# A delta-rule scan with a routed feed-forward: key products in two PSUM banks of their own, a new order of work in a slot

## Chip, cores and metric

The kernel runs on one core of one Trainium2 chip. The metric is the device time of the whole kernel in microseconds; the median of the runs counts. Before the change it is 1098.14 us (three runs, 1096.19 to 1109.95).

## The reference

Three parts follow one another. Only the first one is touched by the change.

```python
# 1. delta rule: 4 batches x 8 heads, 768 steps, head size 48
k_n = k / (norm(k) + 1e-06)
for t in range(S):
    y[:, :, t] = q[t] @ state
    state = state + beta[t] * outer(k_n[t], v[t] - state^T k_n[t])
# 2. top-1 routed feed-forward: 3072 rows of 384, 8 experts of 1024
e = argmax(x @ w_gate); out = softmax_e * (relu(x @ w1[e]) @ w2[e])
# 3. gated unit: (sigmoid(x @ w_gate) * (x @ w_val)) @ w_out, width 1536
```

## The kernel before

All is float32, and matrix products run on PE as several passes. The delta rule is done in chunks: 768 steps are 12 chunks of 64 steps, and 32 (batch, head) pairs lie two by two on the 128 partitions, 16 pairs along the free axis. In each chunk the recurrence is a triangular system of 64 by 64 per pair. It is cut into two blocks of 32 by 32 that are inverted by elimination, and a product that joins them.

Two chunks make a **group** (g = 0 to 5), and each chunk is done in two halves of 8 pairs, so a group has four **slots** (sl = 0 to 3) and the loop of `run` has k = 0 to 25 slots: 24 of the scan and 2 that only finish. The names in the rows:

- `norm(g)` (L83): ACT squares the keys (`sq`), DVE sums them (`n`) and makes `nrm`, `gam`, `ngam` in 17 small instructions.
- `Gd` (L109) and `Gq` (L120): the **key products**, keys with keys (`gd`, 128 matmuls in the trace for a chunk) and keys with queries (`gq`, 64). DVE scales them out of PSUM into `ado` and `atq`, at the place in DVE's order where the call stands.
- `sys`, `lower` (L131, L133): DVE transposes `ado` into `asys`, POOL masks it. `elim` (L138): the elimination, 30 steps of a multiply (L144) and an add (L146). For group 0 DVE does all; for the others POOL does the first 26 and DVE the last JD = 4. `back` (L148) is these last steps and two transposes on DVE, `tn` and `r`.
- `merge` (L157): `mp` and `mr` on PE, copies `pp` and `rt` on ACT, and four copies of the diagonal blocks of `rt` (L181).
- The scan's own steps in slot k: `z_` (PE `zps`, then DVE `z`), `u_` (PE `ups`, then ACT `u` in 8 instructions), `s_` of the slot before (PE `sps`, then DVE adds into the state `S`), `yb` and `ya` (PE `yps`). `rows` (ACT copies the output to `xrow`, a ring of 8), `turn` (PE `xT`, ACT `xt`) and `gate` (PE `lgp`, DVE `lg`) prepare the router.
- `Route.route` (L356) routes four slots at a time: small DVE instructions, `rank` on PE, a scale of each `xrow` on ACT (L396), and on POOL an indirect DMA of each `xrow` to `xs` (L402). Each waits for the one before it to land. It is a generator, moved on by `ra` at three places in a slot.

Each engine works its instructions in the order in which they are written; `pt` moves POOL's elimination on by four instructions at a time, between the other calls. PSUM has eight banks: two for `yps` and six (`ps_m`) that all other products share.

Loads go out on ACT's queue, one or two in a slot. In slot 21 `free_early` gives memory to the weights of the second part, and after the loop the routed part (from about 396 us) and the gated unit keep PE busy to the end.

## Time and profile before

| | |
|---|---|
| median of three runs | 1098.14 us |
| profiled execution, its own time | 1107.87 us |
| its span, first to last instruction | 1106.1 us |
| PE busy in the span | 998.9 us (90%) |
| DVE, ACT, POOL busy | 545.4, 381.3, 373.4 us |
| PE's share of the chain that ended last | 80% |
| granted TensorE clock, mean over the span | 0.900 of full speed |

The clock that is granted to TensorE has two levels here, 1.2 and 2.4 GHz; a row of the stretches gives its mean as a share of 2.4 GHz, so 0.50 is the lower level all the time and 1.00 the upper. A busy PE at the lower level does about half the work, so busy time alone does not tell how fast it is. Times inside the execution are counted from the start of the span.

### The profile page before, as it was taken

The numbers are of one execution on the slowest core, as the hardware profiler recorded it, in microseconds if no ns is written. First come the engines' busy times: TensorE is split into PE (matmuls) and PEld (weight loads), VectorE is DVE, ScalarE is ACT, GpSimd is POOL, SyncE is SP. The second block draws the span as 40 slices with busy tenths as digits, with TensorE's granted clock in tenths as the row PEclk, the third lists the DMA queues.
The fourth block names the chain that finished last, engine by engine and source line by source line (L and its number), as shares of the span: only waits on it lengthen the run. The fifth ranks groups of instructions, "written<-read, shape, count | busy, mean of one in ns | idle before, by whom it ended". The sixth has DMA issues, their size and how long they took to land.

```text
span 1106.1 us, 25856 instructions
## 1 busy us (share of the span) xinstructions
PE 998.9 (90%) x11330; PEld 913.5 (83%) x11330; DVE 545.4 (49%) x1032; ACT 381.3 (34%) x746; POOL 373.4 (34%) x435
## 2 busy tenths in 40 slices
PE   2366989898898899999999999999999999999994
PEld 2355988898797789999999988888888888888894
DVE  6845383747322357656653155553366553343331
ACT  1041526162543344444444433333322222222221
POOL 2048847385701255555566601000010000011211
PEclk8587797878856689999999999999999999999997
DMA  8142132222200164576655312111021100000010
GB/s 316 69 165 80 57 113 82 97 77 72 75 31 31 44 215 130 150 193 195 168 140 161 96 40 76 58 39 48 12 74 58 58 20 1 1 36 29 36 43 32
DMA packets 32029, 94.46 MB, mean 85 GB/s; under 512 B 4168, under 2 KB 12072, under 8 KB 31912
## 3 DMA queue, kind: packets, MB, share of 16 engines
q1 hardware_dynamic: 21384, 61.51, 18.5%
q10 hardware_dynamic: 6624, 21.77, 5.9%
q0 software_dynamic: 3904, 9.47, 2.4%
q8 instruction: 91, 1.49, 0.6%
q14 instruction: 26, 0.21, 0.1%
HBM read 70.90 MB, written 21.84 MB: 84 GB/s over the span
## 4 chain that ended last, share of the span: by engine, by line
PE 80%; DVE 7%; POOL 5%; issue 3%; DMA 2%; ACT 1%; SPq 0%; POOLq 0%; ACTq 0%; DVEq 0%
PE gps L556 5%; PE ops L555 5%; PE gps L557 5%; PE vps L556 5%; PE ops L557 5%; PE vps L555 5%; PE vps L557 5%; PE ops L556 5%; PE gps L555 5%; PE yps L192 4%; PE hps L557 3%; PE hps L555 3%; PE yps L555 3%; PE hps L556 3%; PE yps L556 3%; PE yps L557 3%
## 5 line engine op out<-in xcount | busy, mean ns | idle before, releaser
L472 POOL TENSOR_TENSOR wl<-raw,wh 128x1536 fp32r<-128x1536 f32 x31 | 108.9, 3513 | 82.1 <-ACT wh L471 82.0
L732 DVE TENSOR_TENSOR sg<-vps,sg 128x512 f32<-128x512 f32 (+1 forms) x76 | 50.4, 663 | 162.4 <-PE vps L557 162.4
L592 POOL TENSOR_TENSOR wl<-u,wh 128x512 fp32r<-128x512 f32 x18 | 23.4, 1298 | 246.4 <-ACT wh L591 223.8
L555 PE MATMUL ops<-wh,ph 128*128 128x384 f32 x288 | 97.2, 338 | 0.0
L557 PE MATMUL ops<-wh,pl 128*128 128x384 f32 x288 | 97.2, 338 | 0.0
L556 PE MATMUL ops<-wl,ph 128*128 128x384 f32 x288 | 96.9, 336 | 0.0
L737 ACT CAST ph<-sg 128x512 fp32r<-128x512 f32 (+1 forms) x76 | 45.5, 599 | 143.5 <-DVE sg L732 143.5
L555 PE MATMUL gps<-yh,wh 128*128 128x512 f32 (+1 forms) x228 | 87.1, 382 | 1.2 <-ACT yh L675 1.2
L556 PE MATMUL gps<-yl,wh 128*128 128x512 f32 (+1 forms) x228 | 87.5, 384 | 0.2 <-DVE yl L676 0.2
L556 PE MATMUL vps<-yl,wh 128*128 128x512 f32 (+1 forms) x228 | 87.6, 384 | 0.0
L557 PE MATMUL gps<-yh,wl 128*128 128x512 f32 (+1 forms) x228 | 87.4, 384 | 0.0
L555 PE MATMUL vps<-yh,wh 128*128 128x512 f32 (+1 forms) x228 | 87.4, 383 | 0.0
L557 PE MATMUL vps<-yh,wl 128*128 128x512 f32 (+1 forms) x228 | 87.3, 383 | 0.0
L731 ACT ACTIVATE sg<-gps 128x512 f32<-128x512 f32 (+1 forms) x76 | 43.6, 574 | 116.4 <-PE gps L557 116.4
L703 POOL DMA_INDIRECT out_dram<-acc,idx x24 | 24.5, 1020 | 168.6 <-DVE acc L699 125.3
L146 POOL TENSOR_TENSOR asys<-asys,tmpp 128x130 f32<-128x130 f32 (+14 forms) x130 | 74.0, 569 | 10.2
L738 DVE TENSOR_TENSOR pl<-sg,ph 128x512 fp32r<-128x512 f32 (+1 forms) x76 | 50.4, 663 | 52.7 <-ACT ph L737 52.7
L144 POOL TENSOR_TENSOR tmpp<-asys 128x130 f32<-128x130 f32 (+14 forms) x130 | 68.4, 526 | 9.7
L555 PE MATMUL yps<-hh,wh 128*128 128x432 f32 x192 | 70.4, 367 | 0.0
L555 PE MATMUL hps<-xh,wh 128*128 128x432 f32 x192 | 69.9, 364 | 0.0
L557 PE MATMUL hps<-xh,wl 128*128 128x432 f32 x192 | 69.7, 363 | 0.0
L556 PE MATMUL hps<-xl,wh 128*128 128x432 f32 x192 | 69.1, 360 | 0.0
(179 smaller groups left out, 2292.5 us busy)
## 6 DMA issues: line engine op xcount, KB each, us to landing
raw<-in_we_dram SPq DMA_DIRECT2D x32, 768.0 KB
w<-in_w_dram SPq DMA_DIRECT2D x27, 512.0 KB
f32p<-u SPq DMA_DIRECT2D x27, 256.0 KB
qt<-in_qt_dram ACTq DMA_DIRECT2D x12, 512.0 KB
kt<-in_kt_dram ACTq DMA_DIRECT2D x10, 528.0 KB
xs<-zero SPq DMA_DIRECT2D x8, 648.0 KB
kn<-in_kn_dram ACTq DMA_DIRECT2D x10, 512.0 KB
v<-in_v_dram ACTq DMA_DIRECT2D x12, 384.0 KB
```

What stands on the lines that cost most here:

```text
L144: e.tensor_tensor(out=tv,in0=T[:,j+1:32,j:j+1].to_broadcast([128,n,j]),in1=T[:,j:j+1,0:j].to_broadcast([128,n,j]),op=ALU.mult)
L146: e.tensor_tensor(out=T[:,j+1:32,0:j],in0=T[:,j+1:32,0:j],in1=tv,op=ALU.add)
L192: s.nc.tensor.matmul(ps[r,i],lhsT=lhsT(i,h,r),rhs=rhs[r,i],start=start and i==0,stop=stop and i==7)
L472: eng.tensor_tensor(out=l, in0=t, in1=h.bitcast(F32), op=ALU.subtract)
L555: nc.tensor.matmul(ps, lhsT=lh, rhs=rh, start=first, stop=False)
L556: nc.tensor.matmul(ps, lhsT=lh, rhs=rl, start=False, stop=False)
L557: nc.tensor.matmul(ps, lhsT=ll, rhs=rh, start=False, stop=last)
L703: nc.gpsimd.indirect_dma_start(out=out, out_offset=IO(ap=idx[:, r:r + 1], axis=0), in_=acc[:, r], in_offset=None)
L731: nc.scalar.activation(out=sg, in_=pg_, func=AF.Sigmoid)
L732: nc.vector.tensor_tensor(out=sg, in0=pv, in1=sg, op=ALU.mult)
L737: nc.scalar.copy(out=ph, in_=sg)
L738: nc.vector.tensor_tensor(out=plo, in0=sg, in1=ph.bitcast(F32), op=ALU.subtract)
```

## The change

- `Gd` and `Gq` now only issue matmuls, of both halves of a chunk, into a pool `ps_g` of two PSUM banks; `ps_m` keeps four. A new `Ge` issues the DVE evacuations of all products that are open. It stands behind `z_` and `gate` of a slot, so products made at the end of a slot are evacuated in the next one. In slot 0, and throughout group 0, it also stands right behind a `Gd`.
- The work is dealt out anew over the slots. `norm` of a group goes to slots 2 and 3 two groups and a half ahead (it was slot 0), the last `Gd`, `sys` and one `v` product to slot 0, `turnover` (end of POOL's elimination, mask of the next) and `rows_` (last steps and `tn`) to slot 1, `cols_` (`r`) to slot 2. In group 0 the turn to the next elimination moves from slot 1 to slot 3.
- JD goes from 4 to 2: POOL does 28 steps, DVE two.
- The copies of the diagonal blocks (`diag`) stand apart from `merge`, behind or ahead of it. The add into `S` (`S_`) is a function of its own, issued right behind `s_`. The ring of keys `kn` has 8 buffers for 7, and the loads are issued in other slots.
- The router yields at other places and is moved on by other counts: its scales now fall to slot 3, its first two DMAs to the end of slot 0. In the last slots it is moved on by five steps in mid-slot and to its end at the end of the slot, and `rank` stands behind `sps` and `yps`.

The diff, with the removed lines of the functions left out where the kernel above shows them:

```diff
-JD = 4
+JD = 2
...
-        s.kn=ring("kn",7,[128,NP,64],(0,1,2,5,6))
+        s.kn=ring("kn",8,[128,NP,64],(0,1,4,5,6,7))
...
+    def Gd(s,ch):
+        for x in range(2):
+            ps=s.ps_g.tile([128,8,64],F32,tag="g",name="gd"); s.gps.append((ps,ch,x,0))
+            for i in range(8):
+                for half in range(2):
+                    for h in range(2):
+                        r=64*h+32*half; u=8*x+i
+                        s.nc.tensor.matmul(ps[r:r+32,i],lhsT=s.K(ch,u,h,32*half,32),rhs=s.K(ch,u,h,32*half,64),start=True,stop=True,tile_position=(64*h,r))
+    def Gq(s,ch):
+        for x in range(2):
+            ps=s.ps_g.tile([128,8,64],F32,tag="g",name="gq"); s.gps.append((ps,ch,x,1))
+            for i in range(8):
                 for h in range(2):
...
+                    u=8*x+i
+                    s.nc.tensor.matmul(ps[64*h:64*h+64,i],lhsT=s.K(ch,u,h),rhs=s.Q(ch,u,h),start=True,stop=True)
+    def Ge(s):
+        todo,s.gps=s.gps,[]
+        for ps,ch,x,w in todo:
+            g=ch//2; c=16*(ch%2)+8*x
+            dst=(s.ado[g%2],s.atq[g%3])[w][:,c:c+8]
+            f=s.mup if w else s.ngam[:,ch,8*x:8*x+8]
+            s.nc.vector.tensor_tensor(out=dst,in0=ps,in1=f.to_broadcast([128,8,64]),op=ALU.mult)
...
+    def rows_(s,g):
+        if g:
+            for _ in s.elim(0,g,j0=31-JD): pass
+        s.nc.vector.transpose(out=s.tn.rearrange("p u i -> p i u"),in_=s.asys[g%2].rearrange("p t i -> p i t"))
+    def cols_(s,g):
+        s.nc.vector.transpose(out=s.r.rearrange("p u t -> p t u"),in_=s.asys[g%2])
...
     def merge(s,c1,c2):
...
+    def diag(s,ch):
+        c=16*(ch%2)
+        for q in range(4):
+            r=slice(32*q,32*q+32); b=32*(q%2)
+            s.nc.scalar.copy(out=s.rt[ch%3][r,:,b:b+32],in_=s.r[r,c:c+16])
...
     def s_(s,k):
+        ch,hb=divmod(k,2)
+        return s.each("sps",lambda i,h,r: s.kn[ch%8][r,8*hb+i],s.u[k%2]) if ch<NCH-1 else None
+    def S_(s,k,ps):
         ch,hb=divmod(k,2); S=s.S[hb]
...
+        if ps is None: return
         if ch: s.nc.vector.tensor_tensor(out=S,in0=ps,in1=S,op=ALU.add)
         else: s.nc.vector.tensor_copy(out=S,in_=ps)
...
     def run(s, ro, idle0, free_early):
...
+        s.Gd(0); s.Ge(); s.Gd(1); s.Ge()
         s.sys(0); s.lower(0)
         for c in (2,3): s.load("k",c); s.load("t",c)
         n1=s.norm(1); adv(n1,2)
         s.load("v",0); s.load("q",0); idle0(range(NE))
...
+        adv(s.elim(0,0)); s.rows_(0); s.cols_(0)
         s.warm(WARM[0],s.tn[:,0:4].rearrange("p u i -> p (u i)"))
         s.w(0); adv(n1)
...
+        s.merge(0,None); s.diag(0); s.load("k",4)
+        s.Gd(2); s.Ge(); s.merge(1,0); s.load("k",5)
+        s.Gd(3); s.Ge(); s.sys(1); s.lower(1)
+        s.load("q",1); s.load("v",1); s.diag(1); s.load("t",4)
+        s.Gq(0); s.Ge()
         s.merge(None,1)
...
+        st=dict(pool=s.elim(1,1,j1=31-JD),rt=[],nm=None)
+        def pt(n=4): adv(st["pool"],n)
+        def turnover(g):
+            adv(st["pool"])
+            if g+1<NG: s.lower(g+1); st["pool"]=s.elim(1,g+1,j1=31-JD)
+        def ra(n):
+            for r in st["rt"]: adv(r,n)
+        def norm(g,n):
+            if g<NG:
+                if st["nm"] is None: st["nm"]=s.norm(g)
+                adv(st["nm"],n)
+                if n>9: st["nm"]=None
         for k in range(NS+2):
...
+            g,sl=divmod(k,4); ch=k//2; m=g+2; M=g+3; pre=m<NG; nxt=g+1<NG; end=k>=NS-3
+            if k<NS: s.z_(k)
             if k>1: ro.gate(k-2)
+            s.Ge(); pt()
+            if sl==3: ra(3)
+            if sl==1: ra(1)
+            if 0<k<=NS: sp=s.s_(k-1); s.S_(k-1,sp); s.yb(k-1); ro.rows(k-1,s.yps)
+            if k<NS: s.load(*(("q",2*g+5),("t",2*g+6),("t",2*g+7),("q",2*g+6))[sl])
+            if k<3: s.load("q",2+k)
+            if k<1: s.load("t",5)
             pt()
...
+            if sl==1 and k>4 and k<NS-2: st["rt"]=st["rt"][-1:]+[ro.route(k-5,4)]
+            if k>=NS-2: st["rt"].append(ro.route(k-2,1))
+            if end: ra(5)
+            elif sl==1: ra(3)
+            elif sl==2: ra(2)
+            if g==0:
+                if sl==0: norm(2,99); s.Gq(1); s.Ge(); s.w(1)
+                if sl==1: s.Gd(4); s.Ge()
+                if sl==2: s.Gd(5); s.Ge(); s.sys(2)
+                if sl==3: s.Gq(4); s.Ge(); turnover(1); s.rows_(1); s.cols_(1); norm(3,99); s.w(2)
+            else:
+                if sl==0 and pre: s.Gd(2*m+1); s.Ge(); s.sys(m)
+                if sl==0 and ch+1<NCH: s.w(ch+1)
+                if sl==1 and pre: s.Gq(2*m+1)
+                if sl==1 and nxt: turnover(g+1); s.rows_(g+1)
+                if sl==2 and nxt: s.cols_(g+1); norm(M,2)
+                if sl==3: norm(M,99)
+                if sl==3 and ch+1<NCH: s.w(ch+1)
+            if k<NS: s.u_(k)
+            if 0<k<=NS: ro.turn(k-1)
+            if k<NS: s.ya(k)
             pt()
...
+            if k<NS: s.load(*(("k",2*g+6),("k",2*g+7),("v",2*g+3),("v",2*g+4))[sl])
+            if k<1: s.load("v",2)
+            if g==0:
+                if 0<sl<3: s.Gq(1+sl)
+                if sl==3: s.merge(2,None); s.diag(2); s.merge(3,2); s.Gd(6)
+            else:
+                if sl==0 and pre: s.Gq(2*m)
+                if sl==0 and g<NG: s.merge(None,2*g+1); s.diag(2*g+1)
+                if sl==1 and g==1: s.Ge(); s.Gq(5)
+                if sl==2 and nxt: s.merge(2*g+2,None); s.diag(2*g+2)
+                if sl==3 and nxt: s.merge(2*g+3,2*g+2)
+                if sl==3 and M<NG: s.Gd(2*M)
+            if end: ra(99)
+            else: ra((2,1,1,1)[sl])
             pt()
             if k==NS-3: free_early()
...
     def route(s, k0, n):
...
-            if b == 1: yield
+            if b % 2 or n == 1: yield
...
-            if b % 2: yield
-        if n > 1:
-            yield
+            if b % 2 or n == 1: yield
...
-    ps_m = P("ps_m", 6, psums, space=PSUM)
+    ps_g = P("ps_g", 2, psums, space=PSUM)
+    ps_m = P("ps_m", 4, psums, space=PSUM)
```

**DVE ahead of z in slot 2 of group 1 (k = 6).** Before, the last instructions that DVE works before the `z` of this slot (`asys` and `tmpd` are the elimination, `lga`, `gn`, `oh` the router):

```order
L146 TENSOR_TENSOR asys_129<-asys_129,tmpd 128x2x29
L144 TENSOR_TENSOR tmpd<-asys_129 128x30
L146 TENSOR_TENSOR asys_129<-asys_129,tmpd 128x30
L154 STREAM_TRANSPOSE tn<-asys_129 128x32x32
L369 TENSOR_TENSOR lga_196<-lg,gm_200 128x32
L370 TENSOR_TENSOR lga_196<-lga_196,edesc 128x32
L185 TENSOR_TENSOR v_98<-v_98,nrm 128x768
L372 TENSOR_REDUCE gn_202<-lga_196 128x4
L373 TENSOR_TENSOR oh<-lga_196,gn_202 128x32
L205 TENSOR_TENSOR z_146<-v_98,zps 128x384
```

After, at the same place:

```order
L390 TENSOR_TENSOR oh<-lga_200,gn_206 128x32
L148 TENSOR_TENSOR tmpd<-asys_133 128x58
L150 TENSOR_TENSOR asys_133<-asys_133,tmpd 128x2x29
L148 TENSOR_TENSOR tmpd<-asys_133 128x30
L150 TENSOR_TENSOR asys_133<-asys_133,tmpd 128x30
L156 STREAM_TRANSPOSE tn<-asys_133 128x32x32
L133 TENSOR_TENSOR atq_128<-gq,mup 128x512 x2
L394 TENSOR_TENSOR cum<-cum,oh 128x8 x2
L210 TENSOR_TENSOR z_150<-v_102,zps 128x384
L371 COPY lg<-lgp 128x8
L133 TENSOR_TENSOR atq_130<-gq,mup 128x512 x2
```

The four elimination steps are two, the product `v` has left this place, most of the router's instructions stand ahead of the elimination, and the transposition `asys<-ado`, which stood just ahead of the rows shown, is a slot earlier; the evacuations `atq` of products made in the slot before now stand behind `z` and `lg`.

**POOL at the end of an elimination (that of group 3, `asys_130` and now `asys_134`).** Before, with the router's DMAs (`xs<-xrow`) and the mask of the next group (`AFFINE_SELECT`):

```order
L146 TENSOR_TENSOR asys_130<-asys_130,tmpp 128x7x24
L402 DMA xs<-xrow_188,posi_204 24576x384
L144 TENSOR_TENSOR tmpp<-asys_130 128x150
L146 TENSOR_TENSOR asys_130<-asys_130,tmpp 128x6x25
L144 TENSOR_TENSOR tmpp<-asys_130 128x130
L146 TENSOR_TENSOR asys_130<-asys_130,tmpp 128x5x26
L402 DMA xs<-xrow_189,posi_204 24576x384
L136 AFFINE_SELECT asys_129<-asys_129 128x1024
L137 MEMSET asys_129 128x32
L402 DMA xs<-xrow_190,posi_204 24576x384
```

After:

```order
L150 TENSOR_TENSOR asys_134<-asys_134,tmpp 128x5x26
L417 DMA xs<-xrow_192,posi_208 24576x384
L417 DMA xs<-xrow_193,posi_208 24576x384
L148 TENSOR_TENSOR tmpp<-asys_134 128x108
L150 TENSOR_TENSOR asys_134<-asys_134,tmpp 128x4x27
L148 TENSOR_TENSOR tmpp<-asys_134 128x84
L150 TENSOR_TENSOR asys_134<-asys_134,tmpp 128x3x28
L417 DMA xs<-xrow_194,posi_208 24576x384
L417 DMA xs<-xrow_195,posi_208 24576x384
L140 AFFINE_SELECT asys_133<-asys_133 128x1024
```

Two more elimination steps (four instructions) stand here, behind two DMAs instead of around them, and all four DMAs now stand ahead of the next mask.

## Rows read from the trace of the kernel before

**Rows 1.** Stretches: us, then busy of PE, PEld, DVE, ACT, POOL, PEclk, DMA, GB/s.

```profile
131.00:384.50 253.50, 225.73 (x5710) 211.80 (x5706) 117.66 (x325) 110.58 (x312) 116.03 (x194) 0.75 0.21 67
...
126.30:160.40 34.10, 30.49 (x1115) 28.64 (x1113) 22.71 (x54) 14.77 (x43) 16.11 (x33) 1.00 0.29 90
160.40:180.90 20.50, 20.35 (x430) 18.85 (x428) 6.84 (x16) 9.28 (x27) 18.23 (x30) 0.50 0.22 74
...
221.80:232.10 10.30, 10.30 (x296) 9.63 (x296) 1.75 (x4) 6.11 (x16) 9.20 (x15) 0.50 0.28 85
...
269.60:279.90 10.30, 10.30 (x293) 9.63 (x291) 1.68 (x4) 6.11 (x16) 9.13 (x15) 0.50 0.11 37
...
296.90:327.70 30.80, 28.86 (x505) 27.05 (x509) 11.50 (x32) 10.66 (x37) 4.46 (x7) 0.50 0.09 29
...
337.90:361.80 23.90, 22.31 (x357) 21.35 (x352) 7.58 (x36) 4.49 (x16) 2.57 (x3) 0.50 0.08 27
```

**Rows 2.** Waits of PE from 131 to 385 us: total us, times, longest.

```profile
PE xT L346 <- ACT xrow L340: 8.7, 5, 3.5
PE rank L381 <- DVE oh L373: 5.6, 4, 1.4
PE ups L198 <- DVE z L205: 5.2, 3, 1.9
```

**Rows 3.** PE in order of time: start, us, instruction, [idle before <- releaser].

```profile
287.86 0.55 PE L346 MATMUL xT<-ident,xrow 128*128 128x128 f32 x3 [0.73 <-ACT xrow L340]
288.34 1.13 PE L192 MATMUL yps<-S,qt 64*64 64x48 f32 x32
289.41 1.20 PE L173 MATMUL mr<-r,pp 32*32 32x32 f32 x64
290.54 1.13 PE L198 MATMUL zps<-S,kt 64*64 64x48 f32 x32
...
294.27 1.10 PE L198 MATMUL ups<-z,rt 64*64 64x48 f32 x32
298.84 0.90 PE L346 MATMUL xT<-ident,xrow 128*128 128x128 f32 x3 [3.47 <-ACT xrow L340]
299.67 1.95 PE L192 MATMUL yps<-S,qt 64*64 64x48 f32 x32
301.42 1.91 PE L198 MATMUL zps<-S,kt 64*64 64x48 f32 x32
...
308.08 1.91 PE L198 MATMUL ups<-z,rt 64*64 64x48 f32 x32
```

**Rows 4.** DVE in order of time, around the z of slot 6.

```profile
155.00 2.10 DVE L154 STREAM_TRANSPOSE tn<-asys 128x1024 f32<-128x1024 f32 x1
...
158.81 0.54 DVE L205 TENSOR_TENSOR z<-v,zps 128x384 f32<-128x384 f32 x1
...
160.40 1.27 DVE L129 TENSOR_TENSOR atq<-gq,mup 128x512 f32<-128x512 f32 x2
```

**Rows 5.** PE in order of time: products, start of slot 4, last matmul behind the scan.

```profile
129.09 2.08 PE L127 MATMUL gq<-qt,kt 64*64 64x64 f32 x64
131.01 1.09 PE L198 MATMUL zps<-S,kt 64*64 64x48 f32 x32
...
139.33 2.15 PE L117 MATMUL gd<-kt 64*32 64x64 f32 x128
...
384.46 0.57 PE L492 MATMUL cnt<-cum,ones 128*128 128x8 f32 x2
```

**Rows 6.** POOL in order of time: two masks, and one DMA of the router.

```profile
68.68 1.27 POOL L136 TENSOR_SCALAR_AFFINE_SELECT asys<-asys 128x1024 f32<-128x1024 f32 x1 [48.33 <-DVE asys L132]
...
101.82 1.27 POOL L136 TENSOR_SCALAR_AFFINE_SELECT asys<-asys 128x1024 f32<-128x1024 f32 x1
...
307.27 0.96 POOL L402 DMA_INDIRECT xs<-xrow,posi  x1 [2.37 <-DMA xs<-xrow,posi]
```

**Rows 7.** ACT in order of time: the copy of an output row.

```profile
298.31 0.48 ACT L340 COPY xrow<-yps 128x384 f32<-128x384 f32 x1 [6.49 <-DMA xs<-xrow,posi]
```

More of the change, by code (lines that the diff above doesn't have):

```diff
@@ L107, in warm @@
         for _ in range(n): s.nc.tensor.matmul(ps,lhsT=s.ident,rhs=s.ident if x is None else x,start=True,stop=True)
-    def Gd(s,ch,x):
-        nc=s.nc; g=ch//2
-        ps=s.ps_m.tile([128,8,64],F32,tag="m",name="gd")
-        for i in range(8):
-            for half in range(2):
-                for h in range(2):
-                    r=64*h+32*half; u=8*x+i
-                    nc.tensor.matmul(ps[r:r+32,i],lhsT=s.K(ch,u,h,32*half,32),rhs=s.K(ch,u,h,32*half,64),start=True,stop=True,tile_position=(64*h,r))
-        c=16*(ch%2)+8*x
-        nc.vector.tensor_tensor(out=s.ado[g%2][:,c:c+8],in0=ps,in1=s.ngam[:,ch,8*x:8*x+8].to_broadcast([128,8,64]),op=ALU.mult)
-    def Gq(s,ch,x):
-        nc=s.nc; g=ch//2
-        ps=s.ps_m.tile([128,8,64],F32,tag="m",name="gq")
-        for i in range(8):
-            for h in range(2):
-                u=8*x+i
-                nc.tensor.matmul(ps[64*h:64*h+64,i],lhsT=s.K(ch,u,h),rhs=s.Q(ch,u,h),start=True,stop=True)
-        c=16*(ch%2)+8*x
-        nc.vector.tensor_tensor(out=s.atq[g%3][:,c:c+8],in0=ps,in1=s.mup.to_broadcast([128,8,64]),op=ALU.mult)
+    def Gd(s,ch):
[10 more added lines that the diff above has]
+            for i in range(8):
+                for h in range(2):
+                    u=8*x+i
[7 more added lines that the diff above has]
+            s.nc.vector.tensor_tensor(out=dst,in0=ps,in1=f.to_broadcast([128,8,64]),op=ALU.mult)
     def sys(s,g):
@@ L147, in elim @@
             yield
-    def back(s,g,parts=(0,1)):
-        nc=s.nc; T=s.asys[g%2]
-        if 0 in parts:
-            if g:
-                for _ in s.elim(0,g,j0=31-JD): pass
-            nc.vector.transpose(out=s.tn.rearrange("p u i -> p i u"),in_=T.rearrange("p t i -> p i t"))
-        if 1 in parts:
-            nc.vector.transpose(out=s.r.rearrange("p u t -> p t u"),in_=T)
+    def rows_(s,g):
[4 more added lines that the diff above has]
+        s.nc.vector.transpose(out=s.r.rearrange("p u t -> p t u"),in_=s.asys[g%2])
     def merge(s,c1,c2):
@@ L177, in merge @@
             for h in range(2): nc.scalar.copy(out=s.rt[c2%3][lo[h],:,32:64],in_=m2[lo[h]])
-        if c1 is not None:
-            for q in range(4):
-                r=slice(32*q,32*q+32); b=32*(q%2)
-                nc.scalar.copy(out=rt[r,:,b:b+32],in_=s.r[r,c:c+16])
+    def diag(s,ch):
[3 more added lines that the diff above has]
+            s.nc.scalar.copy(out=s.rt[ch%3][r,:,b:b+32],in_=s.r[r,c:c+16])
     def w(s,ch):
@@ L234, in run @@
         adv(s.norm(0))
-        for ch in range(2):
-            for x in range(2): s.Gd(ch,x)
+        s.Gd(0); s.Ge(); s.Gd(1); s.Ge()
         s.sys(0); s.lower(0)
@@ L240, in run @@
         s.load("v",0); s.load("q",0); idle0(range(NE))
-        adv(s.elim(0,0)); s.back(0)
+        adv(s.elim(0,0)); s.rows_(0); s.cols_(0)
         s.warm(WARM[0],s.tn[:,0:4].rearrange("p u i -> p (u i)"))
         s.w(0); adv(n1)
-        s.merge(0,None)
-        for x in range(2): s.Gd(2,x)
-        s.load("k",4)
-        s.merge(1,0)
-        s.load("k",5)
-        for x in range(2): s.Gd(3,x)
-        s.sys(1); s.lower(1); pool=s.elim(1,1,j1=31-JD)
-        s.load("q",1); s.load("v",1)
-        for x in range(2): s.Gq(0,x)
@@ L301, in run @@
             pt()
             if k==NS-3: free_early()
-        ra(99)
 class Route:
```

55 lines of the change are left out of this document (5 added, 50 removed).

## The prediction

> **What bounds the kernel now.** I read the stretches first, then PE's waits, then the order of time on PE and on the engine that each wait names. The routed part and the gated unit keep PE busy from about 400 us on and the change leaves them alone, so all of it is decided before. In slot 4 the scan gets into its stride: its zps starts at 131.0, and the last matmul behind the scan at 384.5 [rows 5]. In these 253.5 us PE is busy for 225.7, so it waits for 27.8, and its clock has a mean of 0.75 [rows 1]. With two levels, 0.50 and 1.00, that is half of the time, 127 us, at the lower one.
>
> What the lower level costs is read off two slots. A bare slot (zps, lgp, sps, yps, ups, xT, yps) at the upper level takes 290.54 to 294.27 for the first four, 3.73, then 1.10 for ups, 0.48 for xT (287.86 to 288.34) and 1.07 for the second yps (to 289.41): 6.4 us. At the lower level it is 301.42 to 308.08, 6.66, then 1.91, 0.83 (298.84 to 299.67) and 1.75 (to 301.42): 11.15 us [rows 3]. So a microsecond at the lower level gives 0.57 of a microsecond's work and costs 0.43; 127 of them cost some 50, about twice what the waits do themselves.
>
> The two hang together. The wait of ups for DVE's z comes three times, 5.2 us in all and 1.9 at the longest; xT waits five times for ACT's copy of an output row, 8.7 in all and 3.5 at the longest; rank waits four times for DVE, 5.6 in all [rows 2]. The lower level sets in behind such waits: stretches of 20.5, 10.3 and 10.3 us behind the three waits for z, 30.8 and 23.9 behind the two long waits for xT [rows 1]. Shorter waits need not do that: from 126.3 to 160.4 PE was at the upper level throughout, though it idled 34.1 - 30.5 = 3.6 us in it [rows 1].
>
> **The change part by part.**
>
> *Wait for z.* DVE's z of slot 6 runs at 158.81, behind tn (2.10) and v [rows 4]. The order shows why it is late: the transposition into asys, eight elimination instructions, tn, router and v all stand in one slot ahead of it. After the change asys is a slot earlier, four elimination instructions and v are gone from there, and the waits of DVE for gq right behind the matmuls become evacuations that are due a slot later. In slot 1, at the upper level, DVE has lg, two evacuations, S, the router, four steps, tn and cum ahead of z. I estimate 8 to 9 us from its instructions, as long as the slot (6.4 and a gq of 2.08 [rows 3, 5]), and u follows z on PE only 3.7 us later. So these waits go: -5.2, bounds 0 and -5.2. This holds as long as POOL is done with its 28 steps.
>
> *POOL.* Its first elimination of 26 steps lies between the masks at 68.68 and 101.82 [rows 6], 31.7 us without the mask, 1.22 a step. Two more steps cost 1.8 (they are shorter than the mean) to 2.4. A DMA of the router takes 0.96 and then 2.37 of waiting until the next [rows 6], so four take 13.3, part of it beside the two last steps. A group costs POOL about 1.4 + 33.5 + 11.5 = 46 us. PE at the upper level needs about 39 for a group with all its products (four bare slots of 6.4, two gd of 2.15, two gq of 2.08 and four merges of 1.20 [rows 3, 5]), so POOL is the next to be late. It has a lead: its second elimination starts at about 104, its fifth would end at about 104 + 35 + 46 + 46 + 41 = 272, when the scan is in slot 17. At my pace PE gets there at about the same time: 0, bounds 0 and +6.
>
> *Rows of the router.* The 3.47 us wait of xT is ACT's copy at 298.31, which itself waited 6.49 for a DMA of the same ring buffer [rows 3, 7]. Scales and DMAs now come one to two slots earlier, so the copy finds its buffer free. What is left is ACT's queue in slot 3, where two pp, four diag copies and two scales stand ahead of the row: up to the 0.73 seen at 287.86 [rows 3], in five groups. -8.7 + 3.7 = -5. The rank of four slots now has half a slot for its DVE steps; of its 5.6 I take off 3, since the single ones in the last slots still follow a chain on DVE.
>
> *New waits.* In slot 2 of groups 1 and 2 the second sq waits for DVE's n, which now stands behind r, and ACT's u is behind that sq. I price it like a wait for z, 1.9 [rows 2], twice, bounds 0 and 3.8 each. Two banks for the products mean that a Gd in slot 0 waits for the evacuations of the one before; these stand directly behind lg, and PE has sps and yps to do meanwhile: 0.5 in all, bounds 0 and 15 (below). Waits together: -5.2 - 5 - 3 + 3.8 + 0.5 = -8.9, and I take -8, bounds 0 and -20.
>
> *Start.* Group 0 no longer waits in slot 1 for POOL, but in slot 3, with norm(3), both transpositions and v in one piece on DVE and u behind an sq. I put the start of slot 4 at 126 instead of 131.0 [rows 5]: -5, bounds +2 and -9. In this place PE still stands for some microseconds.
>
> *Clock.* The five stretches named add up to 20.5 + 10.3 + 10.3 + 30.8 + 23.9 = 95.8 us [rows 1]. I give back two of 10.3 for the sq waits, and one of 27 (between 30.8 and 23.9) because these two, the longest, lie in slots without gd and gq. 127 - 95.8 + 47.6 = 79 us remain; 48 fewer at 0.43 are -21. Bounds: 0 when it falls as often as now, -50 when never.
>
> *At no cost:* two steps fewer on DVE, 8 buffers for kn, other load slots (each tile is still loaded most of a group ahead of its use) and the separate diag hide beside PE's matmuls; were that cover gone, they would show as waits of under 1 us each.
>
> Sum: -8 - 5 - 21 = -34. It is made against the profiled execution, 1107.87 us (span 1106.1 and 1.8 around it), so 1074. That execution lies 9.7 above the median of 1098.14, and I take the same difference off the median: **1064 us**.
>
> **The rivals.**
>
> *POOL sets the pace.* If the clock hardly falls, PE catches up with POOL in slot 17 and z of slot 18 cannot come before about 275 (272 and 3.5 for steps, tn and z). From there six bare slots (38), four merges (5), an estimated 8 for the last two slots and 6 of waits end at 332 instead of 384.5: -52, **1046**. For it speaks the removal of all long waits, against it the two sq waits.
>
> *The clock falls as often as before.* Then only waits and start count, -13: **1085**. For it: the stretches of the lower level are long (30.8 us with PE busy for 28.9 [rows 1]), so one wait of the wrong length per group is enough.
>
> *Slower: the two banks.* If DVE is late with the evacuations, PE waits in front of each half of a key product; with 12 products left and 1.27 for the two evacuations of one [rows 4] that is up to 15 us. If each such wait brings the clock down, the lower level lasts for some 210 us of the scan: (210 - 127) x 0.43 = +36. With the other terms, -13 + 15 + 36 = +38: **1136**. It decides from the point where about 157 us are at the lower level: then the 13 us are eaten up. Against it: the evacuations stand behind only two DVE instructions.
> The Trainium skill (TensorE: Matmul & The Clock Gate, section "A second HAM failure mode: psum-queue depth-cycling") says that a kernel that cycles its products through PSUM banks leaves PE idle briefly between groups of matmuls, and that its clock then swings between the levels. By that rule the time would be this rival's, 1136. The trace so far bears out the swinging, but not for the shortest waits, as the stretch from 126.3 shows.
>
> **How the numbers follow.** The forecast has 0.50 (1045 to 1080), POOL's pace 0.16, the clock as before 0.23 (1078 to 1100), the slower rival 0.11. The range leaves out the slower rival and the last of POOL's pace: 1034 to 1096. A measurement of this kernel tells about 2%, 22 us, from no change. Faster by that is below 1076: most of the forecast and all of POOL's pace, 0.61. Within 2%: the rest of the forecast and the third case, 0.29. Slower: 0.10.
>
> **What would show it.** In the profile after: no wait of ups for DVE's z, at most one xT wait over 1 us, zps of slot 4 at 122 to 130, and a mean clock of 0.8 to 0.85 from there to the end of the scan. POOL's pace would show as DVE waiting for POOL's asys in slot 1 of the last groups; the two banks as waits of gd and gq for ado and atq. I am wrong if the waits go and the clock stays at 0.75, or if a new wait of 2 us or more comes in every group.

## The result

The changed kernel takes 1065.97 us (median of 4 runs, 1059.22 to 1092.41); the kernel before, on the same chip, 1102.68 (1096.19 to 1109.95). The ratio is 0.965 with a 95% interval of 0.956 to 0.974: faster by 3.5%. A copy of the changed kernel, run later with the first experiments, gave 1074.54 (1065.61 to 1079.83) and 0.980 (0.971 to 0.989). By these two the change is worth 2 to 3.5%, with intervals that reach from 1 to 4.4%. 1064 was forecast.

The ratios leave out runs that lie over 1.5% above the fastest of their kernel; the profiles of the changed kernel (1092.41, span 1090.5), of e1_nolag and of e3_split are of such runs, the copy's (span 1063.7) is not, so both are read. The span splits where zps of slot 4 begins, at zps of slot 16, at the last rank and at the first hps. From the stretches of the three kernels (us, then busy of PE, PEld, DVE, ACT, POOL, PEclk, DMA share, GB/s): before,

```profile
131.01:282.05 151.04, 137.49 (x3999) 129.15 (x3997) 87.24 (x205) 67.17 (x186) 88.85 (x156) 0.82 0.26 84
282.05:384.04 101.99, 87.78 (x1716) 82.18 (x1712) 30.33 (x120) 43.12 (x126) 26.87 (x38) 0.66 0.13 43
```

the changed kernel,

```profile
125.39:259.71 134.32, 122.49 (x3901) 115.73 (x3896) 85.36 (x176) 65.28 (x181) 101.80 (x180) 0.92 0.27 83
259.71:362.23 102.52, 97.45 (x1718) 91.53 (x1710) 29.46 (x115) 44.19 (x127) 29.52 (x43) 0.58 0.15 52
263.50:307.90 44.40, 44.40 (x737) 42.30 (x737) 14.02 (x36) 16.50 (x46) 16.61 (x27) 0.50 0.21 69
```

and its copy.

```profile
122.91:258.34 135.43, 123.40 (x3902) 116.04 (x3897) 83.05 (x176) 65.18 (x181) 104.14 (x184) 0.92 0.27 83
258.34:336.06 77.72, 70.83 (x1718) 66.29 (x1710) 28.56 (x115) 44.09 (x127) 29.07 (x41) 0.85 0.19 67
```

"Low" is the time at the lower level, worked out as 2 x (1 - PEclk) x length; "idle" is length minus PE's busy time. The same for every kernel that was run (the names are explained below):

| kernel | slot 4 at | slots 4 to 16 (idle, low) | slot 16 to last rank (idle, low) | last rank to first hps | span |
|---|---|---|---|---|---|
| before | 131.0 | 151.0 (13.6, 54) | 102.0 (14.2, 69) | 15.0 | 1106.1 |
| changed | 125.4 | 134.3 (11.8, 21) | 102.5 (5.1, 86) | 20.9 | 1090.5 |
| e1_copy | 122.9 | 135.4 (12.0, 22) | 77.7 (6.9, 23) | 20.8 | 1063.7 |
| e1_nolag | 121.2 | 132.8 (11.1, 16) | 102.8 (5.0, 86) | 20.8 | 1084.9 |
| e1_jd4 | 128.0 | 152.4 (15.2, 55) | 77.2 (6.8, 23) | 21.0 | 1086.3 |
| e1_router | 125.2 | 133.3 (7.6, 27) | 79.8 (6.8, 29) | 13.7 | 1058.5 |
| e2_jd2only | 133.8 | 149.6 (11.9, 51) | 91.4 (13.6, 44) | 13.8 | 1099.2 |
| e2_memset | 126.2 | 133.2 (12.1, 13) | 82.6 (9.2, 28) | 18.3 | 1067.6 |
| e2_warm | 125.6 | 133.5 (11.6, 16) | 87.4 (7.6, 21) | 13.0 | 1065.5 |
| e2_sq | 123.9 | 133.3 (11.1, 19) | 78.3 (8.4, 20) | 13.7 | 1059.3 |
| e3_pile | 126.9 | 163.4 (21.4, 69) | 74.9 (5.9, 20) | 20.8 | 1093.2 |
| e3_split | 124.3 | 138.9 (5.0, 42) | 93.7 (4.5, 66) | 20.9 | 1084.6 |
| e3_own6 | 121.3 | 127.3 (9.8, 10) | 91.1 (5.4, 60) | 12.1 | 1060.3 |
| e4_pile2 | 124.7 | 136.4 (15.5, 14) | 88.3 (6.3, 48) | 20.9 | 1077.3 |

Behind the first hps all of them need 706 to 711. In each of the two stages the length follows from the other two figures: with the idle time counted in full, a least-squares line through these rows gives 114.6 + idle + 0.42 x low for slots 4 to 16, within 1.8 us for all, and 61.0 + idle + 0.42 x low for the second, within 2.4 us (without e2_warm, which has extra work there). So a microsecond at the lower level costs 0.42; 0.43 had been read off two slots [rows 3].

Where the time went, before against copy: start -8.1, idle 27.8 to 18.9 = -8.9, low 124 to 45 at 0.42 = -33, hand-over to the routed part +5.8: -44, against a span shorter by 42.4. In the changed kernel's own profile the idle time is 16.9 (-10.9) and the start -5.6, but low is still 107: -7. From slot 16 on it holds two stretches of 44.4 us at the lower level; in the first PE was busy throughout (the third row above), in the second for 42.5. In both profiles the change takes the same waits away; what the clock adds differs. The profile of e3_own6 (1062.11 us) has such a stretch too, of 47.8.

PE's waits in the changed kernel from 125 to 365 us (total us, times, longest) stand against [rows 2]:

```profile
PE gd L117 <- issue: 4.4, 3, 2.3
PE zps L203 <- issue: 2.7, 2, 2.4
PE zps L203 <- ACT u L215: 2.2, 2, 1.2
PE mr L176 <- issue: 2.0, 2, 1.5
PE rank L398 <- DVE oh L390: 1.3, 1, 1.3
PE gq L125 <- issue: 1.2, 1, 1.2
PE gq L125 <- DVE atq L133: 1.2, 1, 1.2
PE xT L363 <- ACT xrow L357: 0.7, 1, 0.7
```

The wait of ups for z is gone, xT fell from 8.7 to 0.7, rank's wait for oh from 5.6 to 1.3. New are the two waits for u, one for atq, and PE waiting for nothing that the profile shows, 10.5 us in all where the kernel before has 4.6. The start of slot 4, then the first products of slot 16 (six of 32, then the rest behind a wait), PE in order of time:

```profile
125.39 1.14 PE L203 MATMUL zps<-S,kt 64*64 64x48 f32 x32
...
259.81 0.34 PE L203 MATMUL zps<-S,kt 64*64 64x48 f32 x6
262.53 0.90 PE L203 MATMUL zps<-S,kt 64*64 64x48 f32 x24 [2.38 <-issue]
```

### The profile page after: what moved, and what is told of

Its sections match the earlier page's. It is cut to its first block, busy times and chain, and to the rows that moved or that the text cites. A ratio compares the mean times of both kernels' runs of the same rounds, so it can differ in the third digit from the quotient of the medians.

```text
span 1090.5 us, 25874 instructions
## 1 busy us (share of the span) xinstructions
PE 986.9 (90%) x11330; PEld 902.8 (83%) x11330; DVE 560.2 (51%) x1012; ACT 381.6 (35%) x746; POOL 380.2 (35%) x455
## 3 DMA queue, kind: packets, MB, share of 16 engines
q1 hardware_dynamic: 21384, 61.51, 18.3%
## 4 chain that ended last, share of the span: by engine, by line
PE 84%; DVE 7%; issue 3%; POOL 2%; ACT 2%; DMA 1%; ACTq 0%; POOLq 0%; DVEq 0%
PE gps L572 5%; PE ops L571 5%; PE gps L573 5%; PE vps L572 5%; PE ops L573 5%; PE vps L571 5%; PE vps L573 5%; PE ops L572 5%; PE gps L571 5%; PE yps L197 5%; PE yps L571 3%; PE yps L572 3%; PE yps L573 3%; PE hps L571 3%; PE hps L573 3%; PE hps L572 3%
## 5 line engine op out<-in xcount | busy, mean ns | idle before, releaser
L571 PE MATMUL vps<-yh,wh 128*128 128x512 f32 (+1 forms) x228 | 87.4, 384 | 0.0
L719 POOL DMA_INDIRECT out_dram<-acc,idx x24 | 23.4, 975 | 169.1 <-DVE acc L715 125.6
L150 POOL TENSOR_TENSOR asys<-asys,tmpp 128x108 f32<-128x108 f32 (+14 forms) x140 | 76.3, 545 | 11.0
L148 POOL TENSOR_TENSOR tmpp<-asys 128x108 f32<-128x108 f32 (+14 forms) x140 | 74.4, 531 | 10.4
```

The lines of the kernel that those rows point to most:

```text
L148: e.tensor_tensor(out=tv,in0=T[:,j+1:32,j:j+1].to_broadcast([128,n,j]),in1=T[:,j:j+1,0:j].to_broadcast([128,n,j]),op=ALU.mult)
L150: e.tensor_tensor(out=T[:,j+1:32,0:j],in0=T[:,j+1:32,0:j],in1=tv,op=ALU.add)
L571: nc.tensor.matmul(ps, lhsT=lh, rhs=rh, start=first, stop=False)
L719: nc.gpsimd.indirect_dma_start(out=out, out_offset=IO(ap=idx[:, r:r + 1], axis=0), in_=acc[:, r], in_offset=None)
```

## The experiments

**One part undone or done alone.** The first four kernels ran on one chip, the copy with them as yardstick.

> The changed kernel as it is, for a second profile and as the yardstick of the three others on the same chip. Theory A (the two stretches of 44.4 us at the lower clock level in slots 18 to 23 are a matter of chance, set off by waits that the profile puts down to nothing): they lie elsewhere or are shorter here, the mean clock from slot 4 to the end of the scan is 0.80 to 0.88 instead of 0.78, and the span is 1057 to 1068. Rival B (slots without gd and gq hold the lower level whatever sets it off): at least 60 us at the lower level between slot 17 and the end of the scan here too.

Measured: 1074.54, ratio 0.980 (0.971 to 0.989), low from slot 16 on 23 us: theory A for this profile, though its mean clock, 0.89, lies a little above A's range. The long stretches come and go; e1_nolag's profile has them again (44.4 and 47.8 us).

In e1_nolag DVE evacuates at once, from the shared pool:

```
-ps=s.ps_g.tile([128,8,64],F32,tag="g",name="gd"); s.gps.append((ps,ch,x,0))
+ps=s.ps_m.tile([128,8,64],F32,tag="m",name="gd"); s.gps.append((ps,ch,x,0))
...
+            s.Ge()
...
-    ps_g = P("ps_g", 2, psums, space=PSUM)
-    ps_m = P("ps_m", 4, psums, space=PSUM)
+    ps_m = P("ps_m", 6, psums, space=PSUM)
```

> The key products go back into the one pool of six banks and DVE evacuates each half right behind its matmuls; the order of the rest stays. Theory A (mine: the waits for z went because the elimination steps and v moved away; the evacuation has little to do with it): no wait of ups for z over 1 us, time within 8 us of the changed kernel's copy, about 1066 to 1074. Rival B (the slot's delay is what frees DVE): waits of ups for DVE's z of 1 to 2 us in groups 1 to 3 again, each followed by some 10 us at the lower level, +5 and 0.43 x 30 = +13: about 1084. Rival C (two banks cost something): waits of gd and gq for evacuations go and it is some 5 us faster.

Measured: 1071.66 (1054.15 to 1086.70), ratio 0.963 (0.952 to 0.974): not slower than the copy. No wait of ups for z. Neither zps for u nor gq for atq appears among its waits, and slots 4 to 16 take 132.8 instead of 135.4. The two banks and the slot's delay, taken together, are no part of the gain.

> DVE does the last four inversion steps again and POOL 26. Theory A (mine: POOL had slack either way, and four more DVE instructions of 0.2 us still leave z in time): within 6 us of the copy, 1060 to 1072, no new wait over 1 us. Rival B (the two steps on DVE are what made z late): ups waits for DVE's z by 1 to 2 us in four groups and the clock falls behind each, +6 and 0.43 x 40 = +17: about 1089. Rival C (POOL was about to set the pace): DVE waits less for asys and it is 3 to 6 us faster.

The edit is `JD = 4`. Measured: 1086.55 (1078.78 to 1109.98), ratio 0.990 (0.985 to 0.995), its runs almost all above the copy's: 10 to 12 us lost. Rival B has the price, but the wait came at another instruction. DVE in order of time in slot 9 (start, us, instruction):

```profile
201.74 0.57 DVE L148 TENSOR_TENSOR tmpd<-asys 128x58 f32<-128x58 f32 x1
202.34 0.63 DVE L150 TENSOR_TENSOR asys<-asys,tmpd 128x58 f32<-128x58 f32 x1
...
208.69 0.76 DVE L394 TENSOR_TENSOR cum<-cum,oh 128x8 f32<-128x8 f32 x2
```

PE's rank behind it, with the idle time ahead and its releaser:

```profile
209.31 0.63 PE L399 MATMUL rank<-cum,ones 128*128 128x32 f32 x2 [2.49 <-DVE cum L394]
```

And the stretch that follows, in the columns of the stretches above:

```profile
208.20:228.70 20.50, 19.39 (x394) 18.12 (x398) 12.24 (x34) 9.98 (x28) 16.53 (x28) 0.50 0.29 90
```

The two instructions of this step take 0.57 and 0.63 here, beside POOL's next inversion, and the first of them 0.22 in the copy's slot 17 (row further down), where POOL has just stopped. The eight of the last four steps take 4.1 us (199.71 to 203.82). The four of the changed kernel take 2.5 in slot 13 (240.05 to 242.52), but 1.75 of that is one multiply that ends with POOL's mask; without such company they take 0.9 (280.0 to 280.9 in the copy's slot 17), so what POOL does beside them counts as much as their number. cum, last in the queue, holds rank, and with it all of PE behind. It is not the only new wait: rank waits for cum a second time, 2.8 us, with 20.5 at the lower level behind it as well, and gq once for atq, 3.7. The Trainium skill (GPSIMD Engine Reference, section "1. Specifications") says that GpSimd shares its SBUF interfaces with VectorE, with contention for DVE instructions of two SBUF inputs; both instructions of a step have two, and the trace agrees with 0.57 and 0.63 against 0.22.

> The router advances in the old rhythm (one step behind the first elimination steps, one behind the second half, one at the slot's end, the scales two per step with one step in between), the rest is the changed kernel. Theory A (the earlier scales and DMAs are what freed xT from the output rows): waits of xT for ACT's row of 5 to 9 us in all and of rank of 3 to 5 us come back, and with a stretch at the lower level behind each long one (0.43 x 25 = 11) it is 18 to 25 us above the copy, about 1087. Rival B (the waits come back but the clock is at its lower level in these slots anyway): +8 to +12, about 1076. Rival C (the rows were late because of other work on ACT and POOL): no change, 1060 to 1072.

The edit puts the `ra(...)` counts and the yields of cum and of the scales back, but not the first `ra` of a slot to its place ahead of `sps`. Measured: 1072.31 (1060.44 to 1080.91), ratio 0.976 (0.963 to 0.990): as the copy, rival C. Of PE's waits in e1_router from 121 us on:

```profile
PE rank L395 <- DVE cum L390: 2.6, 2, 1.4
...
PE xT L359 <- ACT xrow L353: 0.2, 1, 0.2
```

xT is not late with the old counts either, so these were not what freed the rows.

The reverse, only `JD = 2` in the kernel before:

> The kernel before with one part of the change: DVE does the last two inversion steps and POOL 28 (instead of four and 26). Theory A (the four elimination instructions are one of several things ahead of z; the transposition into asys, tn and v stay in the slot): the waits of ups for z shrink from 5.2 to some 2 us, the clock falls in fewer groups, slot 4 still starts at 129 to 132: 10 to 15 us below before, about 1082. Rival B (these steps are the change; the reordering gives little): the waits for z are gone and it reaches the changed kernel, 1063 to 1073. Rival C (no part of it works alone): within 6 us of before, 1088 to 1100.

Measured: 1097.97 (1094.94 to 1107.44), ratio 1.003 (1.000 to 1.006): rival C. PE's waits in e2_jd2only from 121 us on:

```profile
PE xT L346 <- ACT xrow L340: 6.1, 5, 3.2
PE rank L381 <- DVE oh L373: 5.8, 4, 1.5
...
PE rank L382 <- DVE cum L377: 3.7, 4, 1.3
PE ups L198 <- DVE z L205: 1.3, 3, 0.7
```

In the kernel before, from 131 to 385 us, rank's wait for cum is

```profile
PE rank L382 <- DVE cum L377: 2.0, 3, 0.9
```

z fell from 5.2 to 1.3, as expected, but rank's wait for cum rose from 2.0 to 3.7, and low from slot 4 to 16 stayed at 51, after 54. Alone the two steps are worth nothing, and the new order without them about 1% (e1_jd4); together 2 to 3.5%. The parts don't add.

**The pile in slot 1.** Two kernels put Gd(2m+1), its evacuation and the transposition into asys back into slot 1, and v behind tn; they differ in where Gq(2m+1) then stands.

```
-if sl==0 and pre: s.Gd(2*m+1); s.Ge(); s.sys(m)
-if sl==0 and ch+1<NCH: s.w(ch+1)
-if sl==1 and pre: s.Gq(2*m+1)
+if sl==0 and pre: s.Gq(2*m+1); s.Ge()      # e3_pile
+if sl==1 and pre: s.Gd(2*m+1); s.Ge(); s.sys(m)
 if sl==1 and nxt: turnover(g+1); s.rows_(g+1)
+if sl==1 and ch+1<NCH: s.w(ch+1)
+if sl==2 and pre: s.Gq(2*m+1)              # e4_pile2
```

> The changed kernel with one piece of the old order back in groups 1 to 4: Gd(2m+1), its evacuation and the transposition into asys stand in slot 1 again, ahead of the last inversion steps, and v behind tn; Gq(2m+1) takes the place in slot 0. Theory A (this pile on DVE ahead of z of slot 2 is what the change took apart, and the clock fell behind the waits that it makes): waits of ups for z or of rank for cum of 4 to 8 us in groups 1 to 3, 45 to 55 us at the lower level from slot 4 to slot 16 where the changed kernel has 20, and 148 to 152 us from slot 4 to slot 16 instead of 134 to 135: about 1085. Rival B (the gain comes from elsewhere, the load order or the router): 133 to 137 us from slot 4 to slot 16 and 1062 to 1076.

Measured: 1099.89 (1089.04 to 1122.05), ratio 0.996 (0.991 to 1.001): the whole gain gone. But its waits of PE (total us, times, longest) hold one that the edit brought in by accident:

```profile
PE gq L125 <- DMA qt<-in_qt_dram: 10.4, 3, 3.5
PE rank L399 <- DVE cum L394: 6.8, 3, 2.5
```

Gq in slot 0 comes before its chunk of q has landed. So the same was done with Gq in slot 2:

> The old pile in slot 1 again, without the late load: Gd(2m+1), its evacuation and the transposition into asys in slot 1 ahead of the last inversion steps, v behind tn, and Gq(2m+1) in slot 2, so that its chunk of q has a slot and more to arrive. Theory A (the pile on DVE makes rank wait for cum, and the clock falls behind that): no wait of gq for qt over 1 us, waits of rank for cum of 4 to 8 us in groups 1 to 3 with a stretch at the lower level of 14 us or more behind each long one, 45 to 60 us at the lower level from slot 4 to slot 16 and 146 to 153 us for them instead of 134: about 1085. Rival B (the late load of qt was what cost the other kernel its time): 133 to 139 us from slot 4 to slot 16, at most 28 us at the lower level, and 1062 to 1076.

Measured: 1076.15 (1071.23 to 1079.49), ratio 0.980 (0.974 to 0.986): rival B, at the upper end of its range. The waits of rank for cum are all there (6.8 in three, the longest 2.6), as expected, yet the clock hardly falls. B's reason, the late load, covers only part: of the 55 us at the lower level by which the two profiles differ, 17 lie at e3_pile's waits for qt, and 41 are what it has more behind rank. Side by side, PE in order of time in e3_pile, with rank of slot 5 and the next gd:

```profile
162.31 0.38 PE L399 MATMUL rank<-cum,ones 128*128 128x32 f32 x2 [2.34 <-DVE cum L394]
...
180.99 1.75 PE L117 MATMUL gd<-kt 64*32 64x64 f32 x99
```

The stretch of e3_pile between them:

```profile
164.20:181.30 17.10, 17.10 (x407) 16.25 (x409) 11.29 (x30) 10.17 (x29) 15.30 (x24) 0.50 0.25 80
```

PE in e4_pile2, rank of slot 9, with gq right behind it:

```profile
198.55 0.41 PE L399 MATMUL rank<-cum,ones 128*128 128x32 f32 x2 [2.50 <-DVE cum L394]
198.89 3.32 PE L125 MATMUL gq<-qt,kt 64*64 64x64 f32 x64
```

The stretch of e4_pile2 behind that wait:

```profile
199.40:202.80 3.40, 3.40 (x70) 3.40 (x68) 2.49 (x3) 0.84 (x1) 2.93 (x7) 0.50 0.02 5
```

Waits of the same size are followed by 17.1, 20.5 and 13.7 us at the lower level in the one, by 3.4 each time in the other. In e4_pile2 gq stands directly behind the wait. In e3_pile the rest of the slot and all of the next come first, without key products; the level rises 0.3 us after the next gd begins, 0.1 us ahead of it, and, the third time, without one. e1_jd4 fits (a slot 2 without products, 20.5 us), and the kernel before does too: the stretches that set in at 221.8 and 269.6 [rows 1] end 0.2 and 0.3 us ahead of the next key product. In slots 16 to 23, which have none, stretches of 44 us and more are found. So in these profiles the stretch goes with what PE runs behind a wait more than with the wait's length.

That is read from the rows; no kernel changed it alone, and it is not shown that the key products are what brings the level back. Where a stretch ends just ahead of a gd or gq, the two merges of the slot, 128 short matmuls in a row, have run right before. In e3_split (below), which pulls these merges apart, two stretches of 17.1 us end about 1 us behind a gd. Nor is it a full account. In the changed kernel two stretches behind the waits for u end after 3.4 and 6.8 us without a product, and in e3_split the same two waits, with the same work right behind them, are followed by these 17.1 us each. In the copy a gd itself goes on behind a wait of 2.2, and 10.2 us follow.

**The clock where no products are.**

> The changed kernel with four additional 128x128 matmuls of the identity behind yps of each of the slots 16 to 23, into a bank of their own; they cost some 0.65 us a slot at the upper level, 5 us in all. Theory A (slots without gd and gq keep PE busy but hold the lower level once it is there; wide products bring the upper one back): at most 12 us at the lower level from slot 16 to the last rank, where the profiles so far have 24 to 85, the spread of the times is smaller, and the median is 0 to 10 us below the copy's. Rival B (the waits set the level, not the kind of products): as much at the lower level as before, and it is 5 us slower.

```
 if k<NS: s.ya(k)
+if 16<=k<NS: s.warm(4)
```

Measured: 1075.15 (1067.33 to 1078.45), ratio 0.983 (0.978 to 0.988); three other kernels on the same chip lie at 0.968, 0.976 and 1.003. No stretch of over 10.2 us from slot 16 on, and the five runs lie within 11 us. But the four matmuls take 1.2 us at the upper level and 2.1 at the lower, not 0.65, some 10 us in eight slots by the formula above, and low at 21 is more than A's 12 and no less than e2_sq's 20. As an edit it loses; whether it rules the 44 us stretches out, one profile can't say.

> The changed kernel with norm's two squares in slot 2 behind ACT's u instead of ahead of it. Theory A (the second square waits for DVE's n behind r, and u of slots 6 and 10 with it): the waits of zps for u (2.2 us, the longest 1.2) are gone, and with them the lower level of 7 us behind each: 2 + 0.43 x 14 = 8 us faster at most, and within the spread of the runs 3 to 8 us, about 1060 to 1068. Rival B (the square is not what u waits for): the waits stay.

The edit moves `norm(M,2)` behind `s.u_(k)`. Measured: 1065.44 (1061.13 to 1073.33), ratio 0.976 (0.969 to 0.983). The waits of zps for u are gone, and a wait of lgp for xt grew from 0.6 to 2.6; idle is 11.1 instead of 12.0. Theory A holds for the wait; in time, nothing that can be told from the copy.

**Waits for nothing that the profile shows.**

> The changed kernel with the two merges of slot 3 pulled apart in groups 1 to 4: the mp of the odd chunk right behind ups, the mr of the even one at the slot's end. Theory A (PE's wait for nothing that the profile shows at the start of slot 16, 2.1 to 2.4 us in all profiles of the new order, is the supply of instructions: two merges give PE 128 short products with their weight loads in about 1.3 us, and the instruction queue brings 16 KB at a time): that wait falls below 1 us, the stretch at the lower level that sets in behind it near 262 us is gone, -2 and 0.43 x 7 = -5 us in all, within the spread of the runs. Rival B (the wait belongs to the place, another queue or a load): still 2 us or more at the first zps of slot 16.

```
 if k<NS: s.u_(k)
+if g and sl==3 and nxt: s.merge(2*g+3,None)
...
-if sl==3 and nxt: s.merge(2*g+3,2*g+2)
+if sl==3 and nxt: s.merge(None,2*g+2)
```

Measured: 1082.81 (1068.13 to 1086.45), ratio 0.977 (0.969 to 0.985). At zps of slot 16 PE no longer waits. Of its waits in e3_split from 125 to 366 us:

```profile
PE lgp L371 <- issue: 1.8, 1, 1.8
PE gd L117 <- issue: 1.6, 2, 0.9
...
PE zps L203 <- issue: 0.4, 1, 0.4
```

The 0.4 is in slot 13. The 1.8 is in slot 17, one slot behind the place where the wait used to be, and the lower level sets in right behind it at 274.5:

```profile
273.83 0.73 PE L371 MATMUL lgp<-wg,xt 128*128 128x8 f32 x6 [1.83 <-issue]
```

So theory A holds for the place only: the wait shrank and moved. Idle from slot 4 to 16 falls from 12 to 5.0, the lowest of all. It bought nothing: low rose to 42, with 17.1 us behind each of the two waits for u (1.06 and 1.13) that cost 6.8 at most in the changed kernel and its copy.

**The hand-over to the routed part.** In the changed kernel, DVE in order of time behind the last cnt:

```profile
364.94 9.08 DVE L516 CAST exci<-exc 1x8 int32<-1x8 f32 x1
```

POOL at the same time:

```profile
365.12 8.87 POOL L551 MEMSET yT<- 128x10512 f32 x1
```

PE, with what it waits for ahead of the first hps:

```profile
382.47 0.98 PE L559 MATMUL xps<-ident,X 108*128 108x108 f32 x4 [10.39 <-DVE xl L562]
```

In the kernel before, the same cast on DVE:

```profile
386.75 0.17 DVE L500 CAST exci<-exc 1x8 int32<-1x8 f32 x1
```

and the same memset on POOL:

```profile
391.05 8.88 POOL L535 MEMSET yT<- 128x10512 f32 x1
```

POOL used to be behind with its scatters (the last began at 390.09) and came to the memset after DVE's cast; in the changed kernel's profile its last scatter begins at 364.16, and the cast of eight numbers lasts as long as the memset. ACT reads exci, so the weights' split and PE's xps follow late.

> The changed kernel with one instruction moved: POOL clears yT behind the first scatter of the token numbers instead of ahead of it, so not while DVE works out exci and adj. Theory A (DVE's cast into exci took 9.08 us because POOL's memset of 8.87 ran at the same time; in the kernel before POOL got to the memset later): exci and adj take 0.2 us, from the last cnt to the first hps it is 13 to 14 us instead of 19.8, the rest as in the copy: 6 us faster, about 1060 to 1068. Rival B (the cast waits for something else that ends with it): exci still takes 8 to 9 us, or the first hps waits for the weights' split instead, and the time is the copy's.

```
-    nc.gpsimd.memset(yT, 0.0)
...
                 tok_scatter(3 * e + f // 3)
+                if e == 0 and f == 0:
+                    nc.gpsimd.memset(yT, 0.0)
```

Measured: 1064.44 (1059.58 to 1087.82), ratio 0.968 (0.962 to 0.975). The cast on DVE in e2_memset:

```profile
344.77 0.15 DVE L516 CAST exci<-exc 1x8 int32<-1x8 f32 x1
```

PE in e2_memset ahead of the first hps:

```profile
356.94 0.98 PE L558 MATMUL xps<-ident,X 108*128 108x108 f32 x4 [4.76 <-DMA X<-xs]
```

The cast is short, but this profile alone does not show that the moved memset is the reason. POOL's last scatter came late in it,

```profile
348.23 0.96 POOL L417 DMA_INDIRECT xs<-xrow,posi  x1 [2.39 <-DMA xs<-xrow,posi]
```

so the memset would have missed the cast at its old place too. That is what happens in e2_sq, where it stands at the old place. DVE and POOL there:

```profile
338.19 0.20 DVE L517 CAST exci<-exc 1x8 int32<-1x8 f32 x1
```

```profile
341.78 8.88 POOL L552 MEMSET yT<- 128x10512 f32 x1
```

The cause shows in all the profiles together: in the seven in which the memset begins 0.2 us behind the start of the cast, the cast takes 9.07 to 9.12 us; in the seven others it takes 0.15 to 0.40. So a run loses these us or not by the moment at which POOL gets through its scatters; e2_sq and e2_warm hand over in 13.7 and 13.0 with the memset at its old place. In e2_memset the hand-over takes 18.3, since PE waits for X, which waits for the router's late scatters. In time it can't be told from the copy.

> The changed kernel with the key products in the one pool of six banks, evacuated right behind their matmuls, and with POOL's memset of yT behind the first scatter of the token numbers. Theory A (own banks and the slot's delay are worth nothing, they cost the waits of gq for atq and of zps for u, 3 to 4 us): 131 to 134 us from slot 4 to slot 16, 13 to 17 us from the last cnt to the first hps, median 1054 to 1062 and ratio to before 0.960 to 0.968. Rival B (the delay gives what the banks cost): as the kernel with the memset moved, 1060 to 1068, ratio 0.968 to 0.975.

Measured: 1064.63 (1060.81 to 1069.78), ratio 0.969 (0.965 to 0.973): in B's range by the time, though slots 4 to 16 took less than even A had. From slot 4 to 16 it is the fastest of all (127.3), and its hand-over 12.1; but its profile has low 60 from slot 16 on. No version was found that is faster than the changed kernel by more than the spread.

**What stays open.** Undoing the banks with the delay, the router's counts, or the pile (e4_pile2) leaves the time within 3 us of the copy's, and JD = 4 costs 10 to 12. All kernels of the new order start slot 4 earlier, by 3 to 10 us, which JD = 2 alone does not bring (133.8 in e2_jd2only); which part of the order does was not tested. Nor is the rest of the gain traced to one: norm's new place as a whole, the loads and the diagonal copies were not undone.

## Why the prediction was right, and where it was not

**The bound** (idle and low of the scan): right, and so was the price of the lower level, 0.42 against 0.43. Two readings of the rows were loose. Of the three stretches put behind waits for z only the first sets in close behind one (160.4); the others set in at 221.8 and 269.6, 6.7 to 6.8 us after the wait for z ends and 2.8 after a wait of rank for cum. PE in the kernel before:

```profile
215.01 1.14 PE L198 MATMUL ups<-z,rt 64*64 64x48 f32 x32 [1.67 <-DVE z L205]
218.95 0.41 PE L382 MATMUL rank<-cum,ones 128*128 128x32 f32 x2 [0.92 <-DVE cum L377]
```

And the 3.6 us of idling at the upper level from 126.3 to 160.4 hold the first wait for z itself, 1.9; shorter waits make up only 1.7.

**Wait for z** (-5.2): it went, with most of rank's and xT's. That v, asys and the steps ahead of z delayed it, the pile kernels show only in part: with the pile back, PE stands at rank, for cum, and z is no longer what comes last.

**Rows of the router** (-5, and rank -3): xT fell by 8.0 in the changed kernel, 6.5 in the copy, rank's wait for oh by 4.3 and 3.2. The cause given is not borne out: with the old counts back, xT waits 0.2. POOL's four scatters around its last mask begin from 223.8 to 239.3 there and from 225.7 to 240.0 in the changed kernel, so the counts did not bring them forward; whether earlier scatters are what freed the rows was not tested. What the trace offers instead is POOL's mask of the last inversion, in the kernel before:

```profile
255.88 1.26 POOL L136 TENSOR_SCALAR_AFFINE_SELECT asys<-asys 128x1024 f32<-128x1024 f32 x1 [5.26 <-DVE asys L132]
```

and in the changed kernel:

```profile
240.98 1.27 POOL L140 TENSOR_SCALAR_AFFINE_SELECT asys<-asys 128x1024 f32<-128x1024 f32 x1
```

It starts 0.4 us behind the zps of slot 14 before, 2.4 ahead of it after, without waiting for DVE; POOL then comes to the next scatters earlier against the scan. As e4_pile2, with the new rhythm and the late asys, has no xT wait over 0.7 either, each of the two may do; not both were undone in one kernel.

**New waits** (+3.8 for sq, +0.5 for the banks): 2.2 and 1.2 measured, in slots 7 and 11 as foreseen for u. What the sum did not hold is the 6 us more that PE waits for nothing that the profile shows. All together the idle time fell by 8.9 to 10.9, against the 8 taken.

**POOL** (0): right for the time, by little. In the copy DVE waits for it in slot 17. POOL in order of time, a scatter:

```profile
277.23 0.96 POOL L417 DMA_INDIRECT xs<-xrow,posi  x1 [3.10 <-DMA xs<-xrow,posi]
```

DVE's first step there:

```profile
279.95 0.22 DVE L148 TENSOR_TENSOR tmpd<-asys 128x58 f32<-128x58 f32 x1 [3.21 <-POOL asys L150]
```

The estimate of 272 did not see that two scatters stand ahead of POOL's last two steps, which end at 279.9. Rank's 0.4 for cum is all that PE sees of it.

**Start** (-5): -5.6 and -8.1. **At no cost**: held.

**Clock** (-21): the term with the largest error in any one run, -7 in the one profile and -33 in the other. Its sign, a mean clock of 0.80 to 0.85 from slot 4 to the end of the scan, was met by neither: 0.77 in the changed kernel's profile (134.3 us at 0.92 and 102.5 at 0.58), 0.89 in the copy's. The stretches "of 27 us" in slots without products are there, as 44.4 twice or as 20.5 once. "The waits go and the clock stays at 0.75" was a sign of being wrong, and the changed kernel's own profile, with 0.77, comes close to it; the copy's does not.

**The slower rival** failed: gq waits for atq once, 1.2 us. Slots 4 to 16 with two banks against six: 135.4 and 132.8 (e1_copy, e1_nolag), 133.2 and 127.3 (e2_memset, e3_own6). By the rule cited with it (the Trainium skill, TensorE: Matmul & The Clock Gate, section "A second HAM failure mode: psum-queue depth-cycling") cycling through banks should make the clock swing; with two banks against six low is 22 and 16, then 13 and 10, far from the 210 of that rival.

**Missed altogether**: "the change leaves them alone" of the routed part. The code is the same, but in both profiles POOL arrives earlier and its memset falls on DVE's cast: +5.9 and +5.8.

That 1064 came so near to 1066 is in part luck. The gain of the waits was about right; the clock term of -21 lies between two measured ones that are 26 us apart, the hand-over worked against it, and a second set of runs of the same kernel has its median at 1074.54.
